# Softmax sums and their spreads over four groups of rows for batches 1 and 2, and another order of scores in group 0

## The chip, the cores and the metric

The kernel runs on one core of one Trainium2 chip. The metric is the device time of one execution in microseconds (us), the median of several runs.

Engines are named as in the profile: PE is TensorE, which does the matmuls, and PEld its weight loads; DVE is VectorE, ACT ScalarE, POOL GpSimd. PSUM is the memory, in banks, into which matmuls write; SBUF holds the operands. L186 is line 186 of that run's kernel.

## The reference, cut to what matters

Eight batches of 576 tokens with 8 heads of 64 go through attention with a window of 128 and a linear bias. The result, 4608 rows of 512, goes through a gated feed-forward block.

```python
scores = scale * np.matmul(q, k.transpose(0, 1, 3, 2))
mask = (rel >= 0) & (rel < window)
scores = np.where(mask, scores + bias[None], -1000000000.0)
attn = np.exp(scores - np.max(scores, axis=-1, keepdims=True))
attn = attn / (np.sum(attn, axis=-1, keepdims=True) + 1e-09)
x = np.matmul(attn, v)            # then rows of 512: 8 heads of 64
out = (gelu(x @ w_gate) * (x @ w_val)) @ w_out
```

## The kernel before

The 4608 rows are cut into nine groups of 512 for the feed-forward part. While the output matmuls of group g run on PE, the attention of batch g + 1 (for group 0) and of the following ones is woven in between them. A batch's 576 tokens fall into two parts, of 320 and 256 columns. For each part: scores on PE, exp on ACT, a multiply by the mask (with the bias in it) on DVE, the sums over the keys by matmuls with ones on PE, the reciprocal of the sums on DVE, a spread of the reciprocals to 128 partitions by matmuls with 0/1 weights on PE, copies of that from PSUM to SBUF, the values on PE, and the multiply on DVE.

The sums come in two forms. The **wide** form (batches 1 and 2 before the change; the later batches use its sums with a DMA for the spread) puts head pair c into row group c of the PSUM bank, each row group being 32 partitions and one column tile of PE, and all 320 or 256 columns beside one another. Only a few of the 32 rows differ, but the reciprocal pays for every column:

```python
def sums(b, s):
    ps = bank()
    for j, a, e in PIECES[s]:
        for i in (0, 1):
            for c in range(4):
                nc.tensor.matmul(out=ps[32 * c:32 * c + 32, a:e],
                    lhsT=ones[:, min(j, 1), i, :], rhs=prob(b, s, c, i, j, e - a), ...)
    lo, hi = PART[s]
    nc.vector.reciprocal(row(b)[:, lo:hi], ps[:, 0:hi - lo])

def spread_pe(b, s, copies=(nc.scalar.copy, nc.vector.tensor_copy)):
    lo, hi = PART[s]
    pss = [bank() for _ in range(4)]
    for c, ps in enumerate(pss):        # four matmuls of 320 or 256 columns
        nc.tensor.matmul(out=ps[:, 0:hi - lo], lhsT=sel[32 * c:32 * c + 32, 0:2, :]..., ...)
    for c, ps in enumerate(pss):
        copies[c % 2](out=recip[b][:, c, lo:hi], in_=ps[:, 0:hi - lo])
```

The **narrow** form (batch 0 alone, before the change) cuts the columns over the four row groups: 4 x 80 for part 0, and 2 x 128 with two pairs in each for part 1. The reciprocal has 80 or 128 columns. The price is 72 or 32 matmuls for the sums in place of 24, and 16 or 8 for the spread in place of 4 (the traces count two weight loads for each of these float32 matmuls: x32, x16 and x8):

```python
def sums0(s):
    w = WIDE[s]                          # (80, 128)
    ...                                  # todo: head pairs c, i outside, pieces inside
    for c, i, j, a, e in todo:
        for x in range(a // w, (e + w - 1) // w):
            g = x if s == 0 else 2 * x + c // 2      # the row group
            mms.append((g, ...))
    for n, (g, lhsT, rhs, lo, hi) in enumerate(mms):
        nc.tensor.matmul(out=ps[32 * g:32 * g + 32, lo:hi], lhsT=lhsT, rhs=rhs, ...)
    nc.vector.reciprocal(row(0)[:, PART[s][0]:PART[s][0] + w], ps[:, 0:w])
```

The order of work in groups 0 and 1 is a list; numbers are halves of output tiles (six matmuls of 512 columns, 1.4 us), `s2` and `s` are scores, `pv` the values:

```python
0: [("s2", 1), ("s", 1, 0, (0, 1)), 0, 1, ("s", 1, 0, (2, 3)), 2,
    ("s", 1, 1, (0, 1), None, masks), 3, ("sum", 1, 0), ("masks",),
    ("s", 1, 1, (2, 3)), 4, ("spread", 1, 0, (act, act)), 5, ("transposes", 2), ("sum", 1, 1),
    ("pv", 1, 0), 6, ("spread", 1, 1, (act, act)), ("pv", 1, 1), 7],
1: [..., 3, ("sum", 2, 0), ("masks",), ("s", 2, 1, (2, 3)), 4, ("spread", 2, 0), ("s2", 3, masks), 5,
    ("s", 3, 0, (0, 1), None, masks), ("sum", 2, 1), ("pv", 2, 0), 6, ("spread", 2, 1), ...],
```

`s2` of batch 1 takes all four head pairs of token block 2; the last two pairs are transposed on PE and copied by ACT and DVE only just before.

The softmax here doesn't subtract the row's maximum and nothing guards it: scores larger than these inputs give would overflow.

## Time and profile before

| | before |
|---|---|
| median of 3 runs | 358.93 us (358.82 to 359.0) |
| span of the profiled run | 357.4 us, granted clock 1.0 |
| busy: PE / DVE / ACT | 347.6 / 188.7 / 186.0 us |
| PE's waits for the wide reciprocal | 0.8 us, 2 times |

A busy share is an average over the whole span, so it shows that PE is the bound engine but not what a change of one stage is worth. For that, one reads the waits on PE and the distances between the starts of successive steps.

### The profile page before, as it was taken

The numbers are of one execution on the slowest core, as the hardware profiler recorded it, in microseconds if no ns is written. First come the engines' busy times: TensorE is split into PE (matmuls) and PEld (weight loads), VectorE is DVE, ScalarE is ACT, GpSimd is POOL, SyncE is SP. The second block draws the span as 40 slices with busy tenths as digits, with TensorE's granted clock in tenths as the row PEclk, the third lists the DMA queues.
The fourth block names the chain that finished last, engine by engine and source line by source line (L and its number), as shares of the span: only waits on it lengthen the run. The fifth ranks groups of instructions, "written<-read, shape, count | busy, mean of one in ns | idle before, by whom it ended". The sixth has DMA issues, their size and how long they took to land.

```text
span 357.4 us, 7028 instructions
## 1 busy us (share of the span) xinstructions
PE 347.6 (97%) x2811; PEld 174.8 (49%) x2855; DVE 188.7 (53%) x327; ACT 186.0 (52%) x342; POOL 103.5 (29%) x137
## 2 busy tenths in 40 slices
PE   8899999999999999999999999999999999999995
PEld 3668445444454445445454545445444444444443
DVE  5676478434888646656546554745474403403320
ACT  4974495536878366632973287337833133313322
POOL 8853479501930084002910192004000000000000
PEclk9999999999999999999999999999999999999999
DMA  8999999999999199683997499759205020011002
GB/s 95 181 195 196 202 153 198 139 138 184 143 148 179 34 179 177 109 182 63 144 195 168 87 135 199 141 126 93 84 13 132 25 95 1 2 60 57 2 29 88
DMA packets 145888, 42.62 MB, mean 119 GB/s; under 512 B 131608, under 2 KB 138776, under 8 KB 145856
## 3 DMA queue, kind: packets, MB, share of 16 engines
q0 software_dynamic: 106624, 18.88, 70.2%
q1 hardware_dynamic: 36432, 17.31, 21.8%
q10 hardware_dynamic: 2800, 5.99, 7.6%
q8 instruction: 22, 0.36, 0.4%
q14 instruction: 10, 0.08, 0.1%
HBM read 43.65 MB, written 9.53 MB: 149 GB/s over the span
## 4 chain that ended last, share of the span: by engine, by line
PE 89%; DVE 4%; ACT 4%; issue 2%; DVEq 0%; ACTq 0%
PE ps L370 50%; PE ps L393 23%; PE ps L351 5%; PE ps L186 4%; ACT P L193 2%; DVE r L314 2%; PE ps L70 2%; PE ps L308 2%; PE ps L147 1%; PE ps L334 1%; PE ps L407 1%; DVE kT L157 1%; PE ps L292 1%; PE ps L278 0%; DVE hT L377 0%
## 5 line engine op out<-in xcount | busy, mean ns | idle before, releaser
L377 DVE TENSOR_TENSOR hT<-ps,gelu 128x512 bf16<-128x512 f32 (+2 forms) x115 | 74.4, 654 | 108.0 <-PE ps L370 93.1
L376 ACT ACTIVATE gelu<-ps 128x512 bf16<-128x512 f32 (+2 forms) x115 | 65.2, 572 | 115.8 <-PE ps L370 114.6
L370 PE MATMUL ps<-xT,wv 128*128 128x512 bf16 (+2 forms) x453 | 111.4, 366 | 0.6
L370 PE MATMUL ps<-xT,wg 128*128 128x512 bf16 (+2 forms) x444 | 110.4, 366 | 0.8
L393 PE MATMUL ps<-wo,hT 128*128 128x512 bf16 x402 | 94.9, 380 | 0.8
L193 ACT ACTIVATE P<-ps 128x512 bf16<-128x512 f32 x144 | 73.4, 626 | 7.7 <-PE ps L186 7.6
L370 PEld LDWEIGHTS <-wv 128*128 128x128 bf16 x460 | 44.7, 98 | 48.8
L370 PEld LDWEIGHTS <-wg 128*128 128x128 bf16 x460 | 43.2, 98 | 47.1 <-issue 0.3
L196 DVE TENSOR_TENSOR P<-P,emask 128x1024 bf16<-128x1024 bf16 (+1 forms) x79 | 49.0, 641 | 30.7 <-ACT P L193 30.2
L393 PEld LDWEIGHTS <-hT 128*128 128x128 bf16 x420 | 38.8, 98 | 47.9 <-issue 4.0
L99 POOL DMA_DIRECT2D vb<-in_v_dram x40 | 33.9, 882 | 7.8 <-PE ps L370 3.6
L398 ACT COPY osb<-ps 128x512 f32<-128x512 f32 x31 | 18.6, 601 | 29.6 <-PE ps L393 28.7
L590 POOL COPY mark<-hT 1x2 bf16<-1x2 bf16 x4 | 0.7, 176 | 98.8 <-DVE hT L377 98.8
L357 DVE TENSOR_TENSOR xT<-ps,rb 128x320 bf16<-128x320 f32 (+1 forms) x64 | 24.6, 448 | 6.8 <-DMA rb<-rd 2.9
L314 DVE RECIPROCAL r<-ps 128x320 f32<-128x320 f32 (+1 forms) x14 | 26.8, 1936 | 1.4 <-PE ps L308 1.4
L99 POOL DMA_DIRECT2D qs<-in_q_dram x30 | 25.2, 852 | 7.6 <-DMA wo<-in_moe_w_out_dram 5.1
L99 POOL DMA_DIRECT2D ks<-in_k_dram x30 | 25.3, 873 | 1.0 <-DMA qs<-in_q_dram 0.7
L186 PE MATMUL ps<-qT,kT 64*128 64x256 bf16 (+1 forms) x384 | 21.9, 244 | 1.6 <-DVE kT L157 1.1
L186 PEld LDWEIGHTS <-kT 64*128 64x128 bf16 x384 | 13.2, 94 | 13.6 <-issue 10.0
L351 PE MATMUL ps<-P,vb 128*64 128x128 bf16 (+2 forms) x384 | 18.1, 243 | 0.1
L351 PEld LDWEIGHTS <-vb 128*64 128x64 bf16 x384 | 14.7, 110 | 5.2 <-issue 4.8
L70 PE MATMUL ps<-zeros 128*128 128x512 bf16 x24 | 8.8, 485 | 1.3 <-DVE zeros L418 1.2
(65 smaller groups left out, 115.9 us busy)
## 6 DMA issues: line engine op xcount, KB each, us to landing
out_dram<-osb SPq DMA_DIRECT2D x35, 256.0 KB, 3.5
rb<-rd ACTq DMA_DIRECT2D x10, 576.0 KB, 7.3
vb<-in_v_dram POOLq DMA_DIRECT2D x32, 128.0 KB, 7.0
qs<-in_q_dram POOLq DMA_DIRECT2D x24, 128.0 KB, 5.6
ks<-in_k_dram POOLq DMA_DIRECT2D x24, 128.0 KB, 6.1
wo<-in_moe_w_out_dram POOLq DMA_DIRECT2D x2, 768.0 KB, 17.5
wg<-in_moe_w_gate_dram POOLq DMA_DIRECT2D x2, 384.0 KB, 9.5
wv<-in_moe_w_val_dram POOLq DMA_DIRECT2D x2, 384.0 KB, 10.6
```

Of the source, the lines that this page charges most:

```text
L99: nc.gpsimd.dma_start(out=t[lo:128, j, :].rearrange("p (h d) -> p h d", h=H), in_=src[b][:, 128 * j - 64 + lo:128 * j + 64, :].rearrange(" ...
L186: nc.tensor.matmul(out=ps[:, col:col + 128 * n].rearrange("p (n t) -> p n t", n=n), lhsT=blocks(kT, b, i, c, j, 1).rearrange("p n t -> p ( ...
L193: nc.scalar.activation(out=dst, in_=src, func=AF.Exp, scale=0.125)
L196: nc.vector.tensor_tensor(out=dst, in0=dst, in1=m, op=ALU.mult)
L314: nc.vector.reciprocal(row(b)[:, lo:hi], ps[:, 0:hi - lo])
L351: nc.tensor.matmul(out=ps[64 * i:64 * i + 64, a:e], lhsT=vb[b % 2][:, j, 64 * h:64 * h + 64], rhs=prob(b, s, c, i, j, e - a), start=(j == ...
L357: nc.vector.tensor_tensor(out=xT[:, c, b * S + lo:b * S + hi], in0=ps[:, 0:hi - lo], in1=recip[b][:, c, lo:hi], op=ALU.mult)
L370: nc.tensor.matmul(out=ps[:, 0:hi - lo], lhsT=w[:, c, 128 * f:128 * (f + 1)], rhs=xT[:, c, t0 + lo:t0 + hi], start=(c == 0), stop=(c == 3))
L376: nc.scalar.activation(out=gl[:, 0:hi - lo], in_=pg[:, 0:hi - lo], func=AF.Gelu)
L377: nc.vector.tensor_tensor(out=hid[g][:, f, lo:hi], in0=pv[:, 0:hi - lo], in1=gl[:, 0:hi - lo], op=ALU.mult)
L393: nc.tensor.matmul(out=po, lhsT=hid[g][:, f, 128 * t:128 * (t + 1)], rhs=wo[:, f, :], start=(f == 0), stop=(f == NF - 1))
L398: (nc.vector.tensor_copy if g < 2 and t < 2 else nc.scalar.copy)(out=osb, in_=po)
```

## The change

It gives batches 1 and 2 the narrow form, so that their reciprocals are done sooner. It also puts the scores of two head pairs ahead of block 2's in group 0, because those two pairs are transposed well before the other two. `sums0` and `spread0` take the batch as an argument and are called `sums4` and `spread4`; `spread_pe` goes.

```diff
-    def sums0(s):
+    def sums4(b, s):
...
-        nc.vector.reciprocal(row(0)[:, PART[s][0]:PART[s][0] + w], ps[:, 0:w])
+        nc.vector.reciprocal(row(b)[:, PART[s][0]:PART[s][0] + w], ps[:, 0:w])
...
-        0: [("s2", 1), ("s", 1, 0, (0, 1)), 0, 1, ("s", 1, 0, (2, 3)), 2,
-            ("s", 1, 1, (0, 1), None, masks), 3, ("sum", 1, 0), ("masks",),
-            ("s", 1, 1, (2, 3)), 4, ("spread", 1, 0, (act, act)), 5, ("transposes", 2), ("sum", 1, 1),
+        0: [("s", 1, 0, (0, 1)), ("s2", 1), 0, 1, ("s", 1, 0, (2, 3)), 2,
+            ("s", 1, 1, (0, 1), None, masks), 3, ("sum4", 1, 0), ("masks",),
+            ("s", 1, 1, (2, 3)), 4, ("spread", 1, 0, (act, act, act, act)), 5,
+            ("transposes", 2), ("sum4", 1, 1), ("pv", 1, 0), 6,
...
-            ("s", 2, 1, (2, 3)), 4, ("spread", 2, 0), ("s2", 3, masks), 5,
+            ("s", 2, 1, (2, 3)), 4, ("spread", 2, 0, (act, dve, act, dve)), ("s2", 3, masks), 5,
```

## The prediction

> **What bounds the kernel now.** I read the page first (engines, then the chain that ended last), then the list of waits, then the timeline of the three stretches that the change touches: batch 0 (14 to 27 us), batch 1 (44 to 66 us) and batch 2 (86 to 104 us).
>
> ```profile
> span 357.4 us, 7028 instructions
> ...
> PE 347.6 (97%) x2811; PEld 174.8 (49%) x2855; DVE 188.7 (53%) x327; ACT 186.0 (52%) x342; POOL 103.5 (29%) x137
> ...
> PE 89%; DVE 4%; ACT 4%; issue 2%; DVEq 0%; ACTq 0%
> ```
>
> PE has work for 97% of the span; DVE and ACT for about half. The chain that ended last gives DVE 4%, and its list by line gives the wide reciprocal (L314) 2.2%, some 7.9 us. That is not 7.9 us to be had: PE mostly computes other things beside it. What PE really lost to it stands in the list of waits (PE's own, filtered):
>
> ```profile
> PE ps L70 <- DVE zeros L418: 1.2, 1, 1.2
> PE ps L186 <- DVE kT L157: 1.1, 3, 0.5
> PE ps L334 <- DVE r L314: 0.8, 2, 0.4
> PE ps L186 <- DVE xT L357: 0.2, 1, 0.2
> ```
>
> So the change can work on two waits for the reciprocal (L334, 0.4 us each) and on one of 0.5 us for the transposed keys (L186). Everything else on PE is work, and each added nanosecond of PE work ahead of 104 us moves the end by the same, because PE waits for almost nothing later.
>
> The durations of the operations, by form:
>
> ```profile
> L314 DVE RECIPROCAL r<-ps 128x320 f32<-128x320 f32 x7 | 15.1, 2151 | 0.0
> L314 DVE RECIPROCAL r<-ps 128x256 f32<-128x256 f32 x7 | 12.0, 1720 | 1.4 <-PE ps L308 1.4
> L282 DVE RECIPROCAL r<-ps 128x128 f32<-128x128 f32 x1 | 1.0, 958 | 0.6 <-PE ps L278 0.6
> L282 DVE RECIPROCAL r<-ps 128x80 f32<-128x80 f32 x1 | 0.7, 658 | 1.1 <-PE ps L278 1.1
> ```
>
> Batch 0 already uses the new form (L278, L282, L292), so nearly every price can be read off the trace of before. In the timeline (start, duration, engine, line) I take as the price of a step the time from its first weight load to the first weight load of the next step:
>
> ```profile
> 14.44 0.82 PEld L278 LDWEIGHTS <-ones 128*32 128x32 bf16 x72 [0.42 <-issue]
> ...
> 15.32 0.17 PEld L186 LDWEIGHTS <-kT 64*128 64x128 bf16 x6
> ...
> 16.19 0.98 PEld L292 LDWEIGHTS ps<-r,sel 32*128 32x128 f32 x32 [0.42 <-DVE r L282]
> ...
> 17.25 0.97 PEld L351 LDWEIGHTS <-vb 128*64 128x64 bf16 x24
> ```
>
> ```profile
> 53.96 0.51 PEld L308 LDWEIGHTS <-ones 128*32 128x32 bf16 x24 [0.42 <-issue]
> ...
> 54.57 0.39 PEld L186 LDWEIGHTS <-kT 64*128 64x128 bf16 x12
> ...
> 56.97 0.34 PEld L334 LDWEIGHTS ps<-r,sel 32*128 32x128 f32 x8 [0.87 <-ACT P L193]
> ...
> 57.75 0.98 PEld L393 LDWEIGHTS <-hT 128*128 128x128 bf16 x6 [0.44 <-issue]
> ```
>
> The first block is the narrow form in batch 0, the second the wide form in batch 1. The 0.87 us is booked to an exp, but the reciprocal ended at 56.86, 0.11 us before the load; I read it as the wait for the reciprocal, as the chain does.
>
> **What the Trainium skill says.** TensorEngine Tiling (Array Packing), Key Properties: changing the tiling mode drains TensorE. The trace agrees: nearly every change of mode has a gap of 0.42 us in the weight loads, so only what exceeds 0.42 counts as a wait. The change keeps the number of mode changes. TensorE: Matmul & The Clock Gate, Back-to-back issue gap: a floor of some 25 ns for up to 64 columns and 134 cycles (56 ns) for 128. Here 72 sums take 0.88 us, 12 ns each, so tiles in different column groups beat that floor; the 32 of 128 columns take 0.81 us, 25 ns each, about two at a time. VectorE: DVE Perf Modes, Walkthrough: the 8-slice pipeline, has the reciprocal repeating its divide 8 times; at 0.96 GHz that would be 8.3 ns a column, while the trace gives (2151 - 1720) / 64 = 6.7 and (958 - 658) / 48 = 6.3. The measurement decides; either way it is columns that are paid for, and four groups of rows shorten them by 4 (320 to 80) or 2 (256 to 128).
>
> **The change, part by part.**
>
> Reciprocals: per batch 2151 to 658 and 1720 to 958 ns, 2.26 us less DVE; 4.5 us for two batches. All of it lies beside PE work except what PE waits.
>
> The wait at the first spread: in batch 1 the loads before L334 end at 56.10; with the usual 0.42 the spread could start at 56.52 and starts at 56.97: 0.45 us lost. In batch 2 the same (95.63, 96.05, 96.50): 0.45. The new reciprocal ends some 1.2 us sooner (1.49 less, started 0.27 later), so both waits should go: **-0.90 us**.
>
> Sums, part 0: 24 matmuls become 72. 53.96 to 54.57 is 0.61 (0.61 in batch 2), 14.44 to 15.32 is 0.88: +0.27 twice, **+0.54**. Part 1: 24 become 32 of 128 columns, but successive ones lie in the same column group in pairs. 59.15 to 59.78 is 0.63, 0.58 in batch 2; batch 0 takes 24.18 to 24.99, 0.81: +0.18 and +0.23, **+0.41**.
>
> Spreads: the same columns, in four or two rounds with a float32 weight load each. Part 0: 57.00 to 57.76, 0.76, against 16.19 to 17.25, 1.06: +0.30 twice, **+0.60**. Part 1: 0.64 against 0.67: **+0.06**. The copies keep their sizes (400 to 490 ns) and engines.
>
> The new order in group 0: block 2's scores need all four pairs; PE stops in them until the keys of the last pair are copied, and resumes at 46.78 with 10 matmuls to do. From 45.80 to the next step's loads (47.37) is 1.57 us, where the same 16 matmuls take 0.76 in batch 2 (86.14 to 86.90). The new order puts 8 matmuls that need pairs 0 and 1 alone into that hole. It can't end before the keys' copy, so it gains those 8 matmuls, 0.33 to 0.4 us by their loads (0.33 at 50.07), not the whole 0.81: **-0.37**.
>
> Sum: -0.90 + 0.54 + 0.41 + 0.60 + 0.06 - 0.37 = **+0.34 us**. So 358.93 becomes about 359.2.
>
> **The rivals.** (1) The waits matter more than PE's list shows: DVE, 4.5 us lighter, lets masks, evictions and so PSUM banks go sooner, and hidden stalls vanish. For: the chain has 2.2% in L314, and there is a stall of 0.3 us at 103.8 for a copied bank. Against: PE waits for DVE in no other place between 47 and 104 us. It would make some 358.3. (2) A new wait takes the place: each narrow copy in part 1 fills two pairs for half the columns, so the first multiply by the reciprocals needs three ACT copies instead of one, in batch 1 some 0.5 us later (third copy's end about 63.95 against a start of 63.47). Then the last multiply ends near 65.4, while group 1's first projection needs that pair near 66.0. It just holds; were it not to hold, +0.3 us, 359.6. (3) The extra weight loads run dearer than in batch 0, up to double the added 1.6 us: 360.4. Against: batch 0 ran them at full clock, warm, with the same neighbours. (4) Another engine becomes the bound: no, ACT's work is unchanged and DVE's falls.
>
> **Range and chances.** The rivals span 358.3 to 360.4, each with small weight; three runs lie within 0.2 us, and another chip may shift a few tenths. I take 358.2 to 360.1. A move of 2% is 7.2 us; all the PE idle time is 9.8 us (357.4 - 347.6), half of it at start, end and mode changes, and all that is added is 1.6 us. So within 2% is nearly sure.
>
> **What would show it.** Right: reciprocals of about 0.66 and 0.96 us in batches 1 and 2; no wait of L292 for them beyond 0.42; sums and spreads of part 0 at 0.88 and 1.06 us; the step of scores at 46 us some 0.4 shorter, still with a short wait for the keys; group 1's steady state beginning within 0.2 us of before, group 2's 0.2 to 0.5 later, the rest shifted alike. DVE busy 4.5 us lower, without effect. Wrong: a group 2 that begins earlier (the narrow sums were dearer in batch 0 than warm, or rival 1), or a wait of the projections for xT (rival 2).

## The result, and the profile after

| | before | after |
|---|---|---|
| median, 4 runs each | 358.97 us (358.82 to 359.54) | 359.65 us (359.02 to 360.19) |
| span of the profiled run | 357.4 us | 357.8 us |
| busy PE / DVE / ACT | 347.6 / 188.7 / 186.0 us | 351.5 / 184.2 / 185.9 us |

The ratio is 1.0016 (95% interval 0.9996 to 1.0035): the same. A ratio is the mean time of one kernel's fast runs over that of the other's of the same rounds, so it isn't quite the ratio of the medians quoted. The interval holds 1, so these times do not even settle the sign. The profile does.

The head of the page and the chain of work that ended last, after (the chain's shares by engine):

```profile
span 357.8 us, 7414 instructions
...
PE 351.5 (98%) x3031; PEld 177.7 (50%) x3031; DVE 184.2 (51%) x327; ACT 185.9 (52%) x342; POOL 103.5 (29%) x137
...
PE 94%; DMA 2%; POOL 1%; DVE 1%; issue 1%; ACT 0%; POOLq 0%; DVEq 0%; ACTq 0%
```

DVE lost 4.5 us of work, just as worked out, and fell from 4% of the chain to 1%. PE's busy time is not the measure of its cost: 3.9 us more, with more matmul records in this trace (some can be missing, and ends are modelled). PE's own waits, after (us in total, times, longest):

```profile
PE ps L70 <- DVE zeros L406: 1.2, 1, 1.2
PE ps L186 <- DVE kT L157: 0.6, 2, 0.4
PE ps L147 <- DMA vb<-in_k_dram: 0.3, 1, 0.3
PE ps L186 <- DVE xT L345: 0.2, 1, 0.2
```

The wait for the reciprocal is gone from the list, and the one for the keys (kT) is down from 1.1 to 0.6 us. A wait for a load in the first 14 us is new; no line of that part of the kernel was changed. The reciprocals by form (count, then busy us and mean ns of one):

```profile
L314 DVE RECIPROCAL r<-ps 128x320 f32<-128x320 f32 x5 | 10.7, 2147 | 0.0
L314 DVE RECIPROCAL r<-ps 128x256 f32<-128x256 f32 x5 | 8.5, 1705 | 0.0
...
L282 DVE RECIPROCAL r<-ps 128x128 f32<-128x128 f32 x3 | 2.9, 958 | 4.9 <-PE ps L278 4.9
...
L282 DVE RECIPROCAL r<-ps 128x80 f32<-128x80 f32 x3 | 2.0, 657 | 2.0 <-PE ps L278 2.0
```

Two of each form went from 2.15 to 0.66 us and from 1.7 to 0.96. Now PE's weight loads in batch 1, timeline of after (start, duration), to set against the second block in the prediction:

```profile
53.80 0.82 PEld L278 LDWEIGHTS <-ones 128*32 128x32 bf16 x72 [0.42 <-issue]
...
54.69 0.39 PEld L186 LDWEIGHTS <-kT 64*128 64x128 bf16 x12
...
56.64 0.98 PEld L292 LDWEIGHTS ps<-r,sel 32*128 32x128 f32 x32 [0.42 <-ACT P L193]
...
57.70 0.98 PEld L381 LDWEIGHTS <-hT 128*128 128x128 bf16 x6
```

The sums now take 0.89 us (0.61 before), the spread 1.06 (0.78), and between them lie 1.95 us in place of 2.40: the gap ahead of the spread's loads is back to 0.42, as at each of the 14 changes from full tiles (128x128 weights) to smaller ones that this trace has between 45 and 108 us. And the order of scores, before and after:

```profile
45.80 0.34 PEld L186 LDWEIGHTS <-kT 64*128 64x128 bf16 x6
46.77 0.39 PEld L186 LDWEIGHTS <-kT 64*128 64x128 bf16 x10 [0.63 <-DVE kT L157]
47.37 2.27 PEld L393 LDWEIGHTS <-hT 128*128 128x128 bf16 x12 [0.21 <-PE ps L186]
```

```profile
46.06 0.67 PEld L186 LDWEIGHTS <-kT 64*128 64x128 bf16 x14
...
47.03 0.10 PEld L186 LDWEIGHTS <-kT 64*128 64x128 bf16 x2 [0.30 <-DVE kT L157]
47.19 2.27 PEld L381 LDWEIGHTS <-hT 128*128 128x128 bf16 x12
```

Before, ten of the sixteen matmuls stood behind the wait for the keys; after, two. The step shrank from 1.57 to 1.13 us.

**The stretch.** I call the time from the first weight load of batch 1's scores (45.80 before, 46.06 after) to the first weight load of group 2's projections (107.58, 107.98) the stretch. It holds all that was changed: 61.78 us before, 61.92 after. From there to the end both take 249.8 us (357.4 - 107.58 and 357.8 - 107.98). So of the 0.4 us between the two spans only **0.14 us** is the change's doing there; 0.26 arose before any changed instruction had run on PE.

| term, by distances of weight loads | predicted | measured |
|---|---|---|
| order of scores in group 0 | -0.37 | -0.44 |
| sums of part 0, both batches | +0.54 | +0.28 + 0.28 = +0.56 |
| two waits for the reciprocal | -0.90 | -0.45 - 0.46 = -0.91 |
| spreads of part 0 | +0.60 | +0.28 + 0.29 = +0.57 |
| sums of part 1 | +0.41 | +0.18 + 0.22 = +0.40 |
| spreads of part 1 | +0.06 | +0.02 |
| all else | 0 | -0.06 |
| sum | +0.34 | +0.14 |

### The profile page after: what moved, and what is told of

Its sections match the earlier page's. It is cut to its first block, busy times and chain, and to the rows that moved or that the text cites. A ratio compares the mean times of both kernels' runs of the same rounds, so it can differ in the third digit from the quotient of the medians.

```text
span 357.8 us, 7414 instructions
## 1 busy us (share of the span) xinstructions
PE 351.5 (98%) x3031; PEld 177.7 (50%) x3031; DVE 184.2 (51%) x327; ACT 185.9 (52%) x342; POOL 103.5 (29%) x137
## 4 chain that ended last, share of the span: by engine, by line
PE 94%; DMA 2%; POOL 1%; DVE 1%; issue 1%; ACT 0%; POOLq 0%; DVEq 0%; ACTq 0%
PE ps L358 53%; PE ps L381 26%; PE ps L186 4%; PE ps L339 4%; DMA vb<-in_k_dram 2%; PE ps L308 1%; PE ps L292 1%; PE ps L278 1%; PE ps L395 1%; PE ps L147 1%; PE ps L70 0%; POOL ks L123 0%; DVE kT L157 0%; POOL qs L123 0%; DVE xT L345 0%
## 5 line engine op out<-in xcount | busy, mean ns | idle before, releaser
L358 PE MATMUL ps<-xT,wg 128*128 128x512 bf16 (+2 forms) x460 | 112.2, 366 | 0.1
L381 PE MATMUL ps<-wo,hT 128*128 128x512 bf16 x420 | 96.2, 380 | 0.0
L314 DVE RECIPROCAL r<-ps 128x320 f32<-128x320 f32 (+1 forms) x10 | 18.9, 1926 | 0.0
## 6 DMA issues: line engine op xcount, KB each, us to landing
wo<-in_moe_w_out_dram POOLq DMA_DIRECT2D x2, 768.0 KB, 17.5
```

The source lines that it names most:

```text
L358: nc.tensor.matmul(out=ps[:, 0:hi - lo], lhsT=w[:, c, 128 * f:128 * (f + 1)], rhs=xT[:, c, t0 + lo:t0 + hi], start=(c == 0), stop=(c == 3))
L381: nc.tensor.matmul(out=po, lhsT=hid[g][:, f, 128 * t:128 * (t + 1)], rhs=wo[:, f, :], start=(f == 0), stop=(f == NF - 1))
```

## The experiments

All gave correct results. Kernels are compared only within the same rounds.

My theory was that PE is bound throughout and the terms of the table simply add. The rivals were that a lighter VectorE pays somewhere unseen, that the terms depend on each other, and that the start of the kernel became systematically slower.

### swap_only: the order alone

```diff
-        0: [("s2", 1), ("s", 1, 0, (0, 1)), 0, 1,       # kernel before
+        0: [("s", 1, 0, (0, 1)), ("s2", 1), 0, 1,
```

> The kernel before with nothing but the new order in group 0 (two pairs' scores ahead of block 2's). Metric for all runs: the stretch on PE from the first weight load of batch 1's scores to the first weight load of group 2's projections, 61.78 us before and 61.92 with the whole change. My theory (terms add up): the order alone is worth 0.44 us there, so about 61.34, and the whole time about 0.4 us less than before. Rival (the swap gives it back at the bank waits of the next scores, or the changed kernel's waits are coupled): 61.6 or more.

Measured: stretch 45.47 to 106.83, 61.36 us. Median 358.51 us against 359.15 of before; ratio 0.9979 (0.9954 to 1.0004). The order is worth 0.42 us, and nothing is given back.

### narrow_only: the sums and spreads alone

The edit is the reverse of the one above, made in the changed kernel.

> The whole change without the new order. My theory: dearer sums and spreads (+0.56 part 0 sums, +0.40 part 1 sums, +0.57 spreads) against two waits of 0.45 gone, so the stretch grows by some 0.58 us to about 62.36, and the time by as much. Rival (the lighter VectorE pays elsewhere): stretch no longer than before, 61.8.

Measured: stretch 46.05 to 108.39, 62.34 us, 0.56 more than before. Median 359.76 us, ratio 1.0007 (0.9983 to 1.0030). So the narrow form, for which the change was made, costs more PE time than the waits that it removes, and the two parts add: 0.56 - 0.42 = 0.14.

### after_again: the changed kernel once more

> The changed kernel once more, in the same rounds. My theory: the real effect is the stretch's +0.14 us (61.92), and the rest of the 0.4 us between the two profiles is the arrival of a load in the first 14 us, which differs from run to run; so in these rounds a ratio within 1.000 to 1.001. Rival (something systematic in the start makes it slower): the first 14 us again 0.2 us longer than before and a ratio of 1.001 to 1.002.

Measured: stretch 46.39 to 108.31, 61.92 us, the same to the last digit. Median 359.31 us against 359.15, ratio 0.9996 (0.9970 to 1.0022). The start was late again in the profiled run (46.39), but the ratio shows no loss over all runs. Nor was it the same delay: batch 0's sums began at 14.46 us against 14.44 before, and the time was lost after them, ahead of batch 0's first spread (16.77 against 16.19).

The starts explain the scatter. Total span = start + stretch + 249.8, the last being 249.76 to 249.85 us in all profiles of this section. Taking the spans of all runs, the kernel before had starts from 45.4 to 47.9 us in the 11 runs of these rounds, and narrow_part0 from 45.4 to 47.9 as well. That scatter exceeds every effect studied here but that of wide_recip_twice.

### narrow_part0: narrow only where PE had waited

```diff
-("sum4", 1, 1) ... ("spread", 1, 1, (act, act, act, act)) ... ("sum4", 2, 1) ... ("spread", 2, 1, (act, dve, act, dve))
+("sum", 1, 1) ... ("spread1", 1, 1, (act, act)) ... ("sum", 2, 1) ... ("spread1", 2, 1)   # the wide forms
```

> The changed kernel with the wide sums and spreads put back for part 1 of batches 1 and 2, where no wait for the reciprocal was. My theory: the +0.40 us of the part 1 sums goes and nothing comes back, since the wide reciprocal (1.72 us) of part 1 lies beside the values: stretch about 61.50. Rival (the narrow part 1 removed a hidden wait): 61.9 or more.

Measured: stretch 46.03 to 107.52, 61.49 us. Median 358.88 us, ratio 1.0000 (0.9968 to 1.0032). Part 1 of the change bought nothing: no wait was there, and none came back with the wide form.

### interleaved: the narrow sums with neighbours in different row groups

```diff
+        if b > 0:                        # changed kernel, in sums4
+            per = [[m for m in mms if m[0] == g] for g in range(4)]
+            mms = [p[n] for n in range(max(map(len, per))) for p in per if n < len(p)]
         for n, (g, lhsT, rhs, lo, hi) in enumerate(mms):
```

> The changed kernel with the sums of batches 1 and 2 in another order: one matmul of each group of rows in turn. My theory: part 1 (32 of 128 columns, pairs in one column group, 0.81 us) becomes four at a time and falls to some 0.6, and part 0 (72 short ones, 0.88 us) is bound by the number of matmuls, 12 ns each, and stays: stretch about 61.5. Rival: both parts are bound by the number of instructions (part 1 too at 25 ns), no change; second rival: both by collisions in a column group, part 0 falls to 0.65 as well, stretch 61.05.

The timeline of PE's weight loads in batch 1, part 1:

```profile
59.18 0.46 PEld L281 LDWEIGHTS <-ones 128*32 128x32 bf16 x32 [0.42 <-issue]
59.74 0.97 PEld L342 LDWEIGHTS <-vb 128*64 128x64 bf16 x24
```

The 32 matmuls of part 1 fell from 0.81 to 0.56 us in both batches (0.81 and 0.80 before the edit), and are no dearer than the wide form's 24. In the changed kernel the order of these 32, by the code, was row groups 0, 0, 2, 2 over and over for the first half and 1, 1, 3, 3 for the second: pairs, and only two of the four groups at a time. The edit removes both, so which of the two cost the time isn't separated. The 72 of part 0 fell only from 0.89 to 0.84 (11.7 ns each, 0.84 / 72). That the number of instructions sets their price, as I expected, is not shown: no two neighbours of theirs shared a row group before the edit, so it had little to remove, and it leaves eight of one group in a row at the end. The stretch was 46.18 to 107.51, 61.33 us, 0.59 less than the changed kernel's. So what the change had paid for the sums of part 1 (0.40 us) was an avoidable order of matmuls. The total time did not show it: median 359.09 us against 358.85, ratio 1.0000 (0.9987 to 1.0014), as its five starts lay at 45.9 to 46.3 us against 45.4 to 45.9 for the nine runs of before on the same chip. In the profiled run the load of batch 0's keys accounts for it: PE's first matmuls on them came at 6.74 us, after a wait of 1.51 us for the load, against 6.36 and 0.83 in the profile of before, and all later steps up to the stretch are late by the same 0.37 to 0.38. Why the load came late, and whether it did in the other four runs, the record doesn't show.

### narrow_recip_twice: a heavier VectorE in the changed kernel

```diff
-        nc.vector.reciprocal(row(b)[:, PART[s][0]:PART[s][0] + w], ps[:, 0:w])
+        for _ in range(1 if b == 0 else 2):
+            nc.vector.reciprocal(row(b)[:, PART[s][0]:PART[s][0] + w], ps[:, 0:w])
```

> The changed kernel with each of its four narrow reciprocals of batches 1 and 2 issued twice: 2 x (0.66 + 0.96) = 3.2 us more for VectorE. My theory: the reciprocals have over 0.66 us of slack before the spreads and VectorE sets nothing else, so the stretch stays 61.9 within 0.1. Rival (a lighter VectorE is worth something elsewhere, so a heavier one costs): 62.2 or more.

Measured, in few runs: stretch 45.71 to 107.68, 61.97 us; 359.66 us (359.26 and 360.06). VectorE did 3 us more and PE lost 0.05. In the changed kernel the reciprocals are off the path.

### wide_recip_twice: the wait of before, enlarged

```diff
-        nc.vector.reciprocal(row(b)[:, lo:hi], ps[:, 0:hi - lo])
+        for _ in range(2 if b in (1, 2) and s == 0 else 1):
+            nc.vector.reciprocal(row(b)[:, lo:hi], ps[:, 0:hi - lo])
```

> The kernel before with the wide reciprocal of part 0 of batches 1 and 2 issued twice, 2.15 us more ahead of each first spread. My theory: PE waits for it there already, so all of it lands on PE: stretch 61.78 + 4.3 = about 66.1, less what the longer pause gives back later. Rival (the wait at the spread is really for an exp's bank, as the profile books it): far less than 4.3.

Measured: 365.16 us (two runs), ratio 1.0173 (1.0154 to 1.0191); stretch 45.67 to 113.38, 67.71 us. From the sums to the end of the spread went from 3.79 to 5.97 us in batch 1 (53.83 to 59.80) and to 5.98 in batch 2 (95.54 to 101.52): 2.2 us each, the whole of the added reciprocal. So the wait is for the reciprocal, and not for the exp that the profile names at PEld. The stretch rose by more than the 4.3 us, though: by 5.93. The wait list and the weight loads at the two spreads:

```profile
PE ps L335 <- DVE r L315: 5.2, 2, 2.6
...
59.02 0.34 PEld L335 LDWEIGHTS ps<-r,sel 32*128 32x128 f32 x8 [3.07 <-issue]
...
100.74 0.34 PEld L335 LDWEIGHTS ps<-r,sel 32*128 32x128 f32 x8 [3.06 <-issue]
```

The windows of the profile (length, busy PE, PEld, DVE, ACT, POOL, granted PE clock, DMA share, GB/s) show what followed each:

```profile
59.80:61.20 1.40, 1.40 (x10) 0.51 (x6) 1.40 (x3) 1.34 (x4) 1.40 (x3) 1.00 2.43 155
101.50:102.00 0.50, 0.50 (x12) 0.31 (x8) 0.50 (x2) 0.42 (x2) 0.00 (x0) 0.60 2.42 154
102.00:104.70 2.70, 2.70 (x8) 0.74 (x6) 1.77 (x4) 1.32 (x4) 0.00 (x0) 0.50 2.06 136
```

After the wait in batch 1 the clock stayed at 1.00. After the one in batch 2 it was halved for some 3 us, and half an output tile took 2.67 us (102.03 to 104.70) in place of 1.40. From the end of that spread to the values went from 2.85 to 4.41 us: 1.56 us more, which I put down to the clock, on top of 4.37; the two make up the 5.93.

### late_spread: the wide form, with PE doing something else meanwhile

```diff
-        0: [("s2", 1), ("s", 1, 0, (0, 1)), ... 4, ("spread", 1, 0, (act, act)), 5,      # kernel before
+        0: [("s", 1, 0, (0, 1)), ("s2", 1), ... 4, 5, ("spread", 1, 0, (act, act)),
-        1: [... 4, ("spread", 2, 0), ("s2", 3, masks), 5,
+        1: [... 4, ("s2", 3, masks), 5, ("spread", 2, 0),
```

> The kernel before with the new order in group 0 and, in place of narrow sums, the first spread of batches 1 and 2 moved behind the next half of an output tile (six matmuls, 1.4 us), so that the wide reciprocal (2.15 us) is done when PE comes to it. My theory: both waits of 0.45 go at no cost, with the order's 0.44: stretch 61.78 - 0.44 - 0.91 = about 60.4, time some 1.3 us under before, faster than both. Rival (a new wait takes the place: banks, or values waiting for later copies): stretch 61.0 or more.

Measured: stretch 45.47 to 106.35, 60.88 us, 0.5 short of what I expected, and median 358.02 us against 358.85, ratio 0.9975 (0.9963 to 0.9988). By the stretch it beats both kernels; by time it beats before in these rounds, if by only 0.25% (late_again below does not confirm that by time). Against swap_only it gained 0.49 us in batch 2 (from the sums of part 0 to the values of part 0: 6.65 to 6.16 us) and nothing in batch 1 (5.82 and 5.82). Its timeline in batch 1:

```profile
53.95 2.16 DVE L314 RECIPROCAL r<-ps 128x320 f32<-128x320 f32 x1
...
56.03 2.43 DVE L196 TENSOR_TENSOR P<-P,emask 128x1024 bf16<-128x1024 bf16 x4
...
57.83 0.30 PE L308 MATMUL ps<-P,ones 128*32 128x128 bf16 x3
...
58.51 0.60 PE L308 MATMUL ps<-P,ones 128*32 128x128 bf16 x21 [0.39 <-DVE P L196]
```

Four masks stand behind the reciprocal on DVE and end at 58.46 us. The sums of part 1 need them, and PE now came early and waited. This is a new wait in the place of the one removed. It suggests that in batch 1 the wide reciprocal has a second way to hold PE up, through the masks; the next run tests that. In the kernel before, the first wait hid the second: the masks ended at 59.20 us, when PE's sums of part 1 (59.15) had only just begun.

### late_narrow1: the same, with a narrow reciprocal where the masks wait

```diff
-("sum", 1, 0) ... ("spread", 1, 0, (act, act))                    # late_spread
+("sum4", 1, 0) ... ("spread", 1, 0, (act, act, act, act))         # narrow and interleaved, batch 1, part 0 only
```

> The late spreads of late_spread for both batches, with the narrow form (interleaved sums) for part 0 of batch 1 alone; all else wide. In late_spread batch 1 gained nothing: its four masks ended at 58.46 us, after the wide reciprocal, and the sums of part 1 waited for them (0.39 us on PE, 1.22 us from 57.82 to 59.04 in place of 0.6). My theory: there the wide reciprocal holds up VectorE's masks, so a narrow one frees them 1.5 us sooner; the wait goes, the sums of part 1 fall back to 0.6 us, and this pays 0.23 (sums) and 0.31 (spread): stretch 60.88 - 0.62 + 0.54 = about 60.8. Rival (the masks are held up by the exps): wait stays, stretch about 61.4.

```profile
54.08 0.66 DVE L285 RECIPROCAL r<-ps 128x80 f32<-128x80 f32 x1
...
54.65 2.54 DVE L196 TENSOR_TENSOR P<-P,emask 128x1024 bf16<-128x1024 bf16 x4
...
58.28 0.63 PE L311 MATMUL ps<-P,ones 128*32 128x128 bf16 x24
58.83 1.18 PE L354 MATMUL ps<-P,vb 128*64 128x192 bf16 x24
```

The masks ended at 57.2 us in place of 58.5, the wait is gone, and the sums of part 1 took 0.56 us in place of 1.22. Stretch 45.38 to 106.14, 60.76 us. Median 357.96 us against 358.99, ratio 0.9979 (0.9953 to 1.0006; runs of both kernels with a start some 2 us late widen it). By the stretch it is the best of all, by 0.12 us over late_spread. So the wide reciprocal did hold PE up through the masks.

### late_again: late_spread on another chip

> late_spread once more in the same rounds, to see whether it stays ahead of the kernel before on another chip: stretch 60.88 again, ratio 0.997 to 0.998.

Measured in the rounds of late_narrow1: stretch 45.75 to 106.63, again 60.88 us. Median 358.40 us, ratio 0.9986 (0.9961 to 1.0010). The stretch repeats; the total again carries the scatter of the start.

The medians below are of different chips (before had 358.97, 359.15, 358.85 and 358.99 us), so compare the stretches, or each ratio with 1.

| kernel | stretch, us | against before | median, us | ratio |
|---|---|---|---|---|
| before | 61.78 | | 358.97 | |
| after | 61.92 | +0.14 | 359.65 | 1.0016 |
| narrow_only | 62.34 | +0.56 | 359.76 | 1.0007 |
| swap_only | 61.36 | -0.42 | 358.51 | 0.9979 |
| narrow_part0 | 61.49 | -0.29 | 358.88 | 1.0000 |
| interleaved | 61.33 | -0.45 | 359.09 | 1.0000 |
| late_spread | 60.88 | -0.90 | 358.02 | 0.9975 |
| late_narrow1 | 60.76 | -1.02 | 357.96 | 0.9979 |

## Why the prediction was right or wrong

The prediction was right in its result: 359.65 us lies within 358.2 to 360.1, and the sum of +0.34 us lies between the +0.14 of the stretch and the +0.68 of the first medians. How near the total came is in part luck: starts scatter by 2.5 us, more than the range is wide, and the range was drawn from three runs that lay within 0.2 us. The single terms are the test, and they held.

- *Waits for the reciprocal, -0.90.* Right, 0.91, and the reading against the profile's label (an exp) was right too: wide_recip_twice put the whole of its added reciprocals on PE.
- *Sums and spreads, +1.61.* Right, 1.55. Prices read from batch 0 carried over to batches 1 and 2 within 0.02 us for each step of part 0. The spreads of part 0 were put 0.04 too high by a slip: 57.00 to 57.76 are starts of matmuls, while 16.19 to 17.25 are weight loads; by weight loads the wide spread takes 0.78, which gives +0.56 against the measured +0.57. That part 1 runs about two at a time fits interleaved: with all four row groups in turn it took 0.56 us.
- *The new order, -0.37.* Right in kind and a little small: 0.44, and 0.42 alone. The reason given, that the hole's end is set by the copy of the keys and only eight matmuls fit, agrees with the wait of 0.30 us that is left.
- *Gaps at changes of mode.* Read too widely. Of 39 changes of tile shape between 45 and 108 us in the trace of before, the 14 out of full tiles had the gap of 0.42 (12) or, with the wait for the reciprocal, 0.87 (2); the changes back into full tiles had 0.16 or 0.21 in nine of 15 cases, 0.44 in one and none that the view shows in five. Both waits of 0.45 lie at changes out of full tiles, so the sum stands.
- *DVE's 4.5 us without effect.* Right for the changed kernel (narrow_recip_twice: 0.05 us for 3 us more).
- *Rival 1 (hidden stalls).* In the changed kernel it fell. But the argument against it, that PE waits for DVE nowhere else between 47 and 104 us, was too strong: late_spread found a second wait behind the first, through the masks of batch 1. A list of waits shows only those that end last.
- *Rival 2 (the copies).* As argued: the multiplies began at 64.12 us in place of 63.47, the last ended at 65.53 (64.12 + 1.41), and the projection, whose fourth matmul alone needs it, began at 65.18; no wait of the projections for it is on PE's list.
- *Rival 3 (dearer instructions).* Fell: the added 1.61 measured 1.55. Its 360.4 doesn't follow from its own words, either: 358.93 + 0.34 + 1.61 is 360.9.
- *What would show it.* Group 2 did begin 0.40 us later in absolute time, within the 0.2 to 0.5 that I gave, but for a wrong share: 0.26 of it was the start. That the start scatters by more than the effect I had not seen, as three runs of before lay within 0.2 us.

What stays open: why starts scatter from 45.4 to 47.9 us, and whether some kernels meet late starts more often (interleaved had 45.9 or more in all five runs; three of after_again's six had less). In the profiles of after and interleaved the time was lost in waits for loads of batch 0.

## What to carry to other kernels

Filling a wait can be cheaper than shortening it: in batch 2, moving the consumer behind 1.4 us of other work cost no extra PE time (-0.49 us), while shortening the producer by 1.49 us cost PE 0.57 us per batch to win 0.45. But look for the next wait right behind the one that you remove: in batch 1 the same move gained nothing until a shorter reciprocal had freed the masks as well. Count what a shorter operation asks of the bound engine before making it, and use the expensive form only where something waits. When several small matmuls go to different column tiles, go round all the tiles in turn.

## What the Trainium skill lacked or had wrong

- TensorE: Matmul & The Clock Gate, Back-to-back issue gap, gives about 25 ns as a floor for a matmul of up to 64 columns and 134 cycles for 128, and doesn't say there that tiles change it. Its Part 3 does have matmuls in different column groups run concurrently, but gives no spacing for a stream of short ones. In four column tiles 72 matmuls of 16 to 80 columns took 11.7 ns each and 32 of 128 columns took 17.5 ns each (0.56 us / 32).
- No page says in so many words that the order over the column tiles matters, though it fits what that Part 3 says: the same 32 matmuls took 0.81 us in pairs over two tiles at a time and 0.56 us with all four tiles in turn.
- TensorE: Matmul & The Clock Gate, Why this matters for your kernels, advises no PE-idle gaps over about 3 us. The runs don't show this wrong: the two pauses of wide_recip_twice, 2.60 us each by the modelled ends of the matmuls and 3.07 and 3.06 us between weight loads, are about that size. One was followed by a granted clock of 0.50 for some 3 us and a loss of 1.6 us, the other by none.
- TensorEngine Tiling (Array Packing), Key Properties, says that a change of mode drains TensorE, without a figure: between 45 and 108 us here, every change from full tiles to smaller ones left a gap of 0.42 us in the weight loads (0.87 with a wait in it), and changes back into full tiles mostly 0.16 to 0.21 us or none that shows.
- VectorE: DVE Perf Modes, Walkthrough: the 8-slice pipeline, has a reciprocal repeat its divide 8 times. The prediction's 8.3 ns a column (8 / 0.96 GHz) is an estimate from that and from the page's clock; the traces have 6.3 to 6.9 ns ((2147 - 1705) / 64 = 6.9 after, (958 - 657) / 48 = 6.3).
